# Attention and a mixture of experts: a quarter of GpSimd's descriptor space, and a second result buffer for the large expert blocks

## The chip, the cores and the metric

The kernel runs on one core of a Trainium2 chip, as one program. The metric is the device time of one execution in microseconds, and the median over runs is what is compared. Before the change it is 880.67 us, the median of 3 runs that lie between 877.47 and 881.1 us.

## The reference

Attention over 8 batches, 12 heads, 448 positions and a head dimension of 64, with scores capped by a tanh, and then a mixture of 8 experts in which each of the 3584 tokens goes to one expert alone. All of it is in float32.

```
scores = cap * tanh(q @ k^T / 8 / cap);  attn = softmax(scores);  x = (attn @ v) as [3584, 768]
expert = argmax(x @ w_gate);  g = softmax(x @ w_gate)[expert]
out[token] = g * (relu(x[token] @ w1[expert]) @ w2[expert])     # w1: 768 x 1024, w2: 1024 x 768
```

## The kernel before

The first half of the program is attention, written out by hand step by step: for each of the 48 pairs of heads TensorE makes scores, ScalarE takes tanh and exp, VectorE and GpSimd add up the denominators. A batch's rows of x go to DRAM (`xd`), and GpSimd scatters the token numbers into lists by expert (`place_d`, the tile `ids`).

The second half is the experts. The tokens are processed in blocks, each of one expert: two early blocks (-1 and -2) that begin while attention ends, then five large blocks of 448 slots (0 to 4) and two small ones of 256 slots (10 and 11). For a block GpSimd issues one gather of token numbers (`load_ids`), 14 gathers of 128 rows of x into `xg` (`load_x`; 8 for a small block) and four gathers of weights, 1.5 MB each (`load_w`). ScalarE and VectorE split each chunk of weights into a high and a low part (`high`, `low`), and x as well (`split_xs`), so that three fast products stand for one in float32. TensorE does `up(j, f)`, 18 products into `ph`, and `down(j, f)`, 18 products into the six PSUM tiles `y` for a large block, for f from 0 to 7. They are interleaved, with `up` two steps ahead of `down`. After each `up`, ScalarE writes the high half of the hidden layer, and VectorE the low half (`hb`, L945 and L946).

When the last `down` of a block is done, `evac(j)` moves `y` to SBUF: six transposes on VectorE into the tile `ys` (L1003). They stand in VectorE's order ahead of the two L946 of the next block, whose `up(0)` and `up(1)` TensorE does in the meantime. `put(j)` is 14 scatters from `ys` to the output in DRAM, issued by GpSimd in between the gathers for the block after next, spread over the next block's steps (`moves`, with `PS` and `XS`; `step` is a small GpSimd copy that holds GpSimd back until a given `hb` is there). So the scatters of block j end late in the following block, and `evac` of that block writes `ys` again.

`ys` has one buffer in the pool `wb`. Blocks -1, -2, 0, 1, 2, 3 and 4 and the last small block write it; block 10 puts its result into `xg`. The pool `wb` is opened when attention is over, over the places of attention's tiles, and holds in this order: `w24`, `w25h`, `ys`, `w26l`, `w25l`, `w26h`, `w27`. Pools on the left side begin behind the descriptor space of GpSimd's DMAs, which takes the first 16,384 bytes of each partition; pools on the right side (`xp`, `xq`, `hw`, `hw2`, `rpool`) are counted from the other end. A tile that lies where an older tile of a closed pool lay waits for that tile's last users (`reuse_waits`).

GpSimd's DMAs rotate through eight completion semaphores. In the built program a DMA waits for the one before it on its semaphore, so at most eight are under way, and an instruction that has to wait for all 14 scatters waits for all eight semaphores, two in each of four event-semaphore instructions.

Of the kernel before, what the change touches and what calls it, by code (L numbers as in the profile page):

```python
# [4 lines left out]
F32 = mybir.dt.float32  # L5
# [18 lines left out]
QB = S // 32  # L24

KM = 384
XW = DM // 4
# [99 lines left out]
def attention_moe(tc, qT, kT, vL, capd, wgL, w1a, w1b, w2a, w2b, cst, cmk, out):  # L127
    nc = tc.nc
# [662 lines left out]
    def large(j):  # L791
        return j < NL
# [109 lines left out]
    m = {}  # L902
# [83 lines left out]
    ys = {}  # L986

    def evac(j, cs=range(2)):
        y = m["y"]
        if cs[0] == 0:  # L990

            ys[j] = (
                ys0
                if j == -1
                else xg.rearrange("p q x -> p (q x)")
                if j == ORDER[-2]
                else m["yo"].tile([128, QB * XW], F32, name="ys")
            )
        o = ys[j]
        if large(j):  # L1000
            ov = o.rearrange("p (q k i) -> p q k i", k=KC, i=32)
            for k in range(KC):
                V.transpose(out=ov[:, :, k, :], in_=y[k][:, 0:LARGE].rearrange("p (q j) -> p q j", j=32))  # L1003
        else:
            ov = o[:, 0 : 2 * DM].rearrange("p (c a k i) -> p c k a i", c=2, a=4, i=32)
            for c in cs:
                for half in range(2):
                    src = y[2 * c + half][:, 0:384].rearrange("p (k a i) -> p k a i", a=4, i=32)
                    dst = ov[:, c, 3 * half : 3 * half + 3]
                    if half == 0:  # L1010
                        A.copy(out=dst, in_=src)
                    else:
                        V.tensor_copy(out=dst, in_=src)
# [202 lines left out]
    wb = m["yo"] = pools("wb", **tw)  # L1216
    w2s[4] = chunk(wb, "w24")
    w25h = wb.tile([128, DM], F32R, name="w25h")
    ys0 = wb.tile([128, QB * XW], F32, name="ys")
    w26l = wb.tile([128, DM], F32R, name="w26l")  # L1220
    w2s[5] = [w25h, wb.tile([128, DM], F32R, name="w25l")]
    w2s[6] = [wb.tile([128, DM], F32R, name="w26h"), w26l]
# [25 lines left out]
    split_w1(2)  # L1248
    down(-1, 7)
    evac(-1)  # L1250
    split_w1(3)
    fill(100)
# [54 lines left out]
    for i, j in enumerate(blocks):  # L1307
# [43 lines left out]
        if n1 is not None:  # L1351
            evac(j)
    evac(j, range(1))
    put(j, range(1))
    for f in range(3, FC):
# [90 lines left out]
```

## Time and profile before

| | |
|---|---|
| median of 3 runs | 880.67 us (877.47 to 881.1) |
| the profiled execution's own time | 879.77 us |
| its span, first to last instruction | 877.8 us |
| busy: TensorE (PE) / VectorE (DVE) / ScalarE (ACT) / GpSimd (POOL) | 830.4 / 556.9 / 483.4 / 460.5 us |
| GpSimd's gathers of x, scatters of results, gathers of weights | 114, 98 + 4, 28 |

The page gives each engine's busy time as a share of the span, then the span in slices, the DMA queues, the chain of work that ended last, and groups of instructions with the idle time of the engine ahead of them and what ended that idle time. Times in a timeline are microseconds from the start of the span. Matmuls are pipelined: one is shown as lasting longer than the distance to the next one's start, so that the distance of the starts is what one costs.

### The profile page before, as it was taken

How to read it: one execution, taken by the hardware profiler on the slowest of the kernel's cores; microseconds unless marked ns; L12 is line 12 of the kernel's file. 1: busy time of each engine (PE TensorE's matmuls, PEld its weight loads, DVE VectorE, ACT ScalarE, POOL GpSimd, SP SyncE). 2: the span in 40 equal slices, each digit the busy share in tenths (PEclk: the TensorE clock that was granted, in tenths of full speed). 3: DMA queues.
4: the chain of work that ended last, by engine and by line, in shares of the span. 5: the costliest groups of instructions: out<-in, count | busy, mean ns of one | idle time of the engine just before them, and what ended most of it. 6: DMA issues, size and time to landing. Idle time of an engine off the chain costs nothing.

```text
span 877.8 us, 12128 instructions
## 1 busy us (share of the span) xinstructions
PE 830.4 (95%) x4492; PEld 555.2 (63%) x4492; DVE 556.9 (63%) x912; ACT 483.4 (55%) x573; POOL 460.5 (52%) x380
## 2 busy tenths in 40 slices
PE   8999999999969999689999999999999999999993
PEld 3233332323222322169999989899999999999993
DVE  3559797979966899958682844734635536437620
ACT  7999998989876989413342532423323324233420
POOL 1423353434347654534348767578577675665710
PEclk9999999999999999899999999999999999999997
DMA  6131545555556655336645272454431124544210
GB/s 211 69 127 66 186 80 172 98 154 101 187 100 200 223 162 136 80 93 163 134 167 206 77 300 61 176 193 165 169 100 55 33 63 175 186 180 166 81 43 34
DMA packets 46883, 117.96 MB, mean 134 GB/s; under 512 B 8241, under 2 KB 27091, under 8 KB 43744
## 3 DMA queue, kind: packets, MB, share of 16 engines
q1 hardware_dynamic: 30688, 57.01, 23.5%
q0 software_dynamic: 15840, 59.86, 19.3%
q8 instruction: 37, 0.61, 0.3%
q14 instruction: 30, 0.25, 0.1%
q10 hardware_dynamic: 288, 0.23, 0.1%
HBM read 101.40 MB, written 22.36 MB: 141 GB/s over the span
## 4 chain that ended last, share of the span: by engine, by line
PE 53%; DVE 8%; issue 4%; POOL 2%; DMA 2%; ACT 1%; POOLq 0%; DVEq 0%; ACTq 0%
PE ph L940 23%; PE y L970 17%; PE y L978 4%; DVE p L282 2%; PE po L320 2%; PE sp L253 2%; DVE ys L1003 1%; PE po L970 1%; PE z L970 1%; DMA idt<-ids,ti 1%; POOL out L812 1%; DMA ids<-tok,slots 1%; DVE xl L917 1%; PE ps_l L970 1%; PE ps_s L970 1%
## 5 line engine op out<-in xcount | busy, mean ns | idle before, releaser
L290 POOL TENSOR_TENSOR p<-p,pr 64x896 f32<-64x896 f32 x47 | 107.3, 2282 | 189.8 <-DVE p L282 114.7
L945 ACT ACTIVATE hb<-ph 128x448 fp32r<-128x448 f32 (+1 forms) x69 | 35.1, 508 | 285.9 <-PE ph L940 197.4
L946 DVE SCALAR_TENSOR_TENSOR hb<-ph,hb 128x448 fp32r<-128x448 f32 (+1 forms) x69 | 39.4, 574 | 191.2 <-ACT hb L945 191.2
L264 ACT ACTIVATE pt<-sp,qsc 128x896 f32<-128x896 f32 x144 | 139.2, 1001 | 33.6 <-PE sp L253 33.0
L802 POOL DMA_INDIRECT xg<-xd,xi x114 | 136.5, 1198 | 37.8 <-issue 31.7
L253 PE MATMUL sp<-qr,kr 64*128 64x448 f32 x576 | 134.9, 572 | 3.0 <-ACT pr L264 1.5
L273 ACT ACTIVATE pt<-pt,capt 128x1792 f32<-128x1792 f32 x94 | 132.9, 1413 | 2.3
L320 PE MATMUL po<-pt,vr 128*64 128x448 f32 x576 | 130.9, 562 | 0.0
L812 POOL DMA_INDIRECT out<-ys,xi x98 | 107.7, 1099 | 29.2 <-issue 27.4
L253 PEld LDWEIGHTS sp<-qr,kr 64*128 64x128 f32 x576 | 47.1, 185 | 85.3 <-issue 46.7
L282 DVE TENSOR_TENSOR p<-pt 128x896 f32<-128x896 f32 x48 | 71.3, 1485 | 31.1 <-ACT pt L273 25.5
L320 PEld LDWEIGHTS po<-pt,vr 128*64 128x64 f32 x576 | 33.2, 137 | 79.3 <-issue 78.8
L282 DVE TENSOR_TENSOR p<-p,pt 128x896 f32<-128x896 f32 x48 | 54.5, 1135 | 20.7 <-ACT pt L273 19.8
L544 POOL DMA_INDIRECT ids<-tok,slots x32 | 36.4, 1136 | 12.6 <-issue 5.8
L913 ACT CAST xh<-xt 128x448 fp32r<-128x448 f32 (+1 forms) x54 | 27.0, 531 | 20.8 <-DVE xt L910 20.7
L336 DVE COPY ot<-po 128x448 f32<-128x448 f32 x48 | 29.5, 615 | 10.4 <-PE po L320 10.2
L309 PE MATMUL po<-pr,vr 64*64 64x448 f32 x192 | 27.3, 570 | 7.1 <-DVE ot L336 7.1
L802 POOL DMA_INDIRECT w1r<-in_w1b,widx x7 | 10.0, 1435 | 44.8 <-DVE w17l L848 44.5
L910 DVE STREAM_TRANSPOSE xt<-xg 128x448 f32<-128x448 f32 (+1 forms) x54 | 30.2, 584 | 0.8
L917 DVE TENSOR_TENSOR xl<-xt,xh 128x448 fp32r<-128x448 f32 (+1 forms) x54 | 28.8, 559 | 0.0
L1003 DVE STREAM_TRANSPOSE ys<-y 128x448 f32<-128x448 f32 x36 | 19.8, 613 | 13.2 <-DMA out<-ys,xi 7.7
L952 POOL COPY pace<-hb 128x1 f32<-128x1 f32 x40 | 13.7, 342 | 27.0 <-ACT hb L945 26.9
(420 smaller groups left out, 1946.1 us busy)
## 6 DMA issues: line engine op xcount, KB each, us to landing
vr<-in_vL SPq DMA_DIRECT2D x24, 448.0 KB, 6.1
kr<-in_kT SPq DMA_DIRECT2D x23, 448.0 KB, 3.4
qr<-in_qT SPq DMA_DIRECT2D x23, 448.0 KB, 4.6
xd<-yt SPq DMA_DIRECT2D x20, 336.0 KB, 6.5
xd<-w2r SPq DMA_DIRECT2D x12, 336.0 KB, 6.8
w1r<-in_w1a SPq DMA_DIRECT2D x8, 384.0 KB, 5.3
w1r<-in_w1b SPq DMA_DIRECT2D x8, 384.0 KB, 5.7
w2r<-in_w2a SPq DMA_DIRECT2D x8, 384.0 KB, 5.6
```

The lines of the kernel that those rows point to most:

```text
L253: PE.matmul(sp[:, j, 0:S], kr[r, i, c], qr[r, i, :], start=True, stop=True)
L264: A.activation(out=x, in_=sp[:, 0:2, 0:S], func=AF.Tanh, scale=qsc)
L273: A.activation(out=pt[:, lo:hi, :], in_=pt[:, lo:hi, :], func=AF.Exp, scale=capt)
L282: V.tensor_tensor(out=p4, in0=pt[:, 0:2] if half == 0 else p4, in1=pt[:, 2 * half + 2 : 2 * half + 4], op=ALU.add)
L290: e.tensor_tensor(out=p4[r], in0=p4[r], in1=rests[n // 2][r], op=ALU.add)
L320: PE.matmul(po[64 * j : 64 * j + 64, 0:S], vr[:, n % 2 * 6 + 3 * j + t, :], pt[:, 2 * t + j], start=n == t == 0, stop=t == 2 and n > 0,)
L802: G.indirect_dma_start(out=dst, out_offset=None, in_=src, in_offset=bass.IndirectOffsetOnAxis(ap=idx.bitcast(U32), axis=0), bounds_check=b ...
L812: i = G.indirect_dma_start(out=dst, out_offset=bass.IndirectOffsetOnAxis(ap=idx.bitcast(U32), axis=0), in_=src, in_offset=None, bounds_che ...
L917: e.tensor_tensor(out=m["xl"][:, k, 0:n], in0=xts.pop((j, k)), in1=m["xh"][:, k, 0:n], op=ALU.subtract)
L940: PE.matmul(ph, w[:, c], x[:, k, 0:n], start=i == 0, stop=i == 3 * KC - 1)
L946: V.scalar_tensor_tensor(out=hl, in0=ph, scalar=0.0, in1=hh, op0=ALU.max, op1=ALU.subtract)
L970: PE.matmul(y[k][:, 0:LARGE], w[:, c], h, start=f == 0 and i == 0, stop=f == FC - 1 and i == 2)
```

## The change

The descriptor space is set to 4096 bytes instead of the default 16,384, and `ys` gets two buffers of 10,752 bytes in the pool `wb`. Both lines that allocate `ys` name the same tile, so that they rotate through the same two buffers.

```
@@ evac @@
-                else m["yo"].tile([128, QB * XW], F32, name="ys")
+                else m["yo"].tile([128, QB * XW], F32, name="ys", bufs=2)
@@ attention_moe, the pool wb @@
-    ys0 = wb.tile([128, QB * XW], F32, name="ys")
+    ys0 = wb.tile([128, QB * XW], F32, name="ys", bufs=2)
@@ kernel @@
-    nc = bacc.Bacc("TRN2", target_bir_lowering=False, num_devices=1)
+    nc = bacc.Bacc("TRN2", target_bir_lowering=False, num_devices=1, dynamic_dma_scratch_size=4096)
```

## Rows read from the trace of the kernel before

**Rows 1.** Stretches: length, each engine's busy time, TensorE clock, DMA share, GB/s
```profile
445.00:868.00 423.00, 415.90 (x2182) 386.97 (x2180) 213.97 (x331) 142.98 (x232) 270.12 (x259) 1.00 0.38 136
562.00:620.00 58.00, 56.88 (x281) 52.32 (x280) 29.33 (x43) 18.72 (x30) 41.04 (x39) 1.00 0.43 155
```

**Rows 2.** TensorE's waits from 430 us on: in total, times, longest
```profile
PE y L970 <- DVE hb L946: 1.9, 2, 1.1
PE y L978 <- DVE hb L946: 1.2, 1, 1.2
PE ph L940 <- DVE xl L917: 0.2, 1, 0.2
```

**Rows 3.** Waits of all engines from 440 to 868 us
```profile
POOL w1r L802 <- DVE w17l L848: 44.5, 6, 8.6
...
DVE ys L1003 <- DMA out<-ys,xi: 7.7, 3, 3.7
...
DVE ys L1003 <- PE ph L940: 2.9, 1, 2.9
```

**Rows 4.** Line 1003's event semaphores at three evacuations: durations in ns, first and last start
```profile
L1003 DVEq EVENT_SEMAPHORE  x4: 50/50/3869, 558.2 to 562.5; - x4
...
L1003 DVEq EVENT_SEMAPHORE  x4: 49/50/3152, 617.8 to 621.2; - x4
...
L1003 DVEq EVENT_SEMAPHORE  x4: 50/50/2101, 792.9 to 794.1; - x4
```

**Rows 5.** Timeline of VectorE at three evacuations: start, us, idle time before in brackets
```profile
501.89 0.95 DVE L848 TENSOR_TENSOR w25l<-w2r,w25h 128x768 fp32r<-128x768 f32 x1
502.76 3.29 DVE L1003 STREAM_TRANSPOSE ys<-y 128x448 f32<-128x448 f32 x6
...
562.59 3.31 DVE L1003 STREAM_TRANSPOSE ys<-y 128x448 f32<-128x448 f32 x6 [3.70 <-DMA out<-ys,xi]
565.82 1.12 DVE L946 SCALAR_TENSOR_TENSOR hb<-ph,hb 128x448 fp32r<-128x448 f32 x2
...
796.29 3.30 DVE L1003 STREAM_TRANSPOSE ys<-y 128x448 f32<-128x448 f32 x6 [2.92 <-PE ph L940]
```

**Rows 6.** Timeline of GpSimd: scatters ahead of the evacuations
```profile
552.95 1.62 POOL L812 DMA_INDIRECT out<-ys,xi  x1 [0.30 <-issue]
...
559.51 0.98 POOL L812 DMA_INDIRECT out<-ys,xi  x1 [0.30 <-issue]
...
793.06 1.15 POOL L812 DMA_INDIRECT out<-ys,xi  x1 [0.30 <-issue]
```

**Rows 7.** Timeline of TensorE at the first products of `down` behind three evacuations
```profile
557.49 0.36 PE L970 MATMUL y<-hb,w27l 128*128 128x448 f32 x1
...
564.98 0.36 PE L970 MATMUL y<-hb,w20h 128*128 128x448 f32 x1
566.46 0.47 PE L970 MATMUL y<-hb,w20h 128*128 128x448 f32 x1 [1.12 <-DVE hb L946]
...
566.97 0.57 PE L970 MATMUL y<-hb,w20h 128*128 128x448 f32 x2
...
624.82 0.80 PE L970 MATMUL y<-hb,w20h 128*128 128x448 f32 x2
...
793.75 0.36 PE L970 MATMUL y<-hb,w27l 128*128 128x448 f32 x1
...
798.45 0.33 PE L978 MATMUL y<-w20l,hb 128*128 128x384 f32 x1
799.96 0.62 PE L978 MATMUL y<-w20h,hb 128*128 128x384 f32 x2 [1.18 <-DVE hb L946]
```

**Rows 8.** DMA issues, us to landing; the last line is that of the `w2` gathers
```profile
xg<-xd,xi POOLq DMA_INDIRECT x114, 3.4
out<-ys,xi POOLq DMA_INDIRECT x98, 2.4
...
DMA to landing us min/median/max: 2.1/9.8/10.3
```

## The prediction, made before the result was known

> **What bounds the kernel now.** I read the stretches first. In the expert part, from 445 us to 868 us, TensorE is busy 415.9 of 423 us at a granted clock of 1.00, that is at its upper level of 2.4 GHz, and no other engine comes near: GpSimd 270 us, VectorE 214 us [rows 1]. So only TensorE's own waits can be got back there. The list of them is the second view: three from VectorE's `hb` (1.9 us in two, 1.2 us in one) and one of 0.2 us from `xl`, 3.3 us in all [rows 2]. Everything that a second result buffer could give has to come out of these and of waits too small to be listed. A GpSimd that waits costs nothing by itself.
>
> The third view is who VectorE waits for. Of its time ahead of the transposes of `evac`, 7.7 us are put down to the scatters out of `ys`, 2.9 us to TensorE [rows 3]. The second needs care. Each evacuation is preceded by four event semaphores, two of the scatters' eight completion counts each; a normal one takes 50 ns, and one took 3869 ns at the evacuation from 558 us, 3152 ns from 618 us, and 2101 ns from 794 us [rows 4]. That is the scatters' wait, whatever name is printed. At 559.51 us GpSimd began the last scatter of block -2 and had issued it by 560.49 us; the transposes began at 562.59 us [rows 5, 6]. At 793.06 us it began the last one of block 3, done issuing at 794.21 us, and the transposes began at 796.29 us: the same distance of 2.1 us. I therefore count the wait at 794 us as one for the scatters too.
>
> **The change part by part.**
>
> *The second buffer takes the scatters' wait away.* `evac(j)` then writes the buffer that block j-2's scatters read, and these were issued a whole block (58 us) earlier; they land in 2.4 us [rows 8]. What is late next, at each place:
>
> At 562 us: the last product into `y` starts at 557.49 us [rows 7], and VectorE has nothing left to do from 558.89 us (562.59 - 3.70) [rows 5]. The transposes, 3.31 us, could run from 558.9 to 562.2 us, and the first `hb`, half of 1.12 us, until about 562.8 us [rows 5]. TensorE needs that `hb` for the second product of `down`. Two such products take 0.57 us and one 0.36 us, so their starts are 0.21 us apart, and it would have started at 564.98 + 0.21 = 565.19 us; it started at 566.46 us [rows 7]. Gain 1.27 us, with over 2 us to spare.
>
> At 621 us: two products took 0.80 us instead of 0.57 us [rows 7], a wait too short to be listed. Gain 0.23 us.
>
> At 796 us: block 10 is small, and its two `up` are shorter, so the same delay hits harder. The product due some 0.18 us after 798.45 us (half its printed length, as above) started at 799.96 us [rows 7]: 1.33 us. Without the scatters' wait the transposes start when `y` is done, at 794.11 us (793.75 + 0.36), and with 3.30 us for them and 0.56 us for the first `hb` it is 797.97 us, ahead of 798.63 us. Gain 1.33 us.
>
> At 502 us nothing goes: VectorE was in `w25l` until 502.84 us (501.89 + 0.95), and the transposes followed at once [rows 5]. The smaller of the two waits that make 1.9 us, 0.8 us, is this one and stays [rows 2]. The other two evacuations into `ys` have no wait of TensorE behind them, and nothing is gained there.
>
> The sum is 1.27 + 0.23 + 1.33 = 2.83 us. Bounds: 0, if something else is late at each place; 3.3 us plus 0.5 us (the unlisted 0.23 us, and starts that slip by more than the listed idle time), if every wait of TensorE in the expert part went. It carries to the end, because between the boundaries TensorE's list has no wait [rows 2] that a boundary's delay could hide in.
>
> *Earlier transposes move what follows them.* The splits of `w17`, `w26` and `w27` behind `evac` come up to 3.4 us earlier, and GpSimd's gather of the next weights, which waits 44.5 us in six times for `w17l` [rows 3], goes with them. Nothing on TensorE was waiting for either; I take 0. The other side: VectorE now works beside the last scatters. A scatter beside VectorE's splits took 1.62 us, one without 0.98 us [rows 6], so one or two of them per block may take 0.64 us longer. GpSimd has 58 - 41 = 17 us to spare in a large block [rows 1], and nobody waits for these scatters any more. Cost 0; if it had no slack, 5 x 1.3 = 6.4 us.
>
> The Trainium skill ("SBUF — State Buffer", section "SBUF: two separate sides") says that GpSimd can't write its descriptors while VectorE runs an operation that takes the shared port pair. That would be the reason for the 1.62 us; by that rule alone the change makes GpSimd's issue slower than before, and the sum would still be the same as long as the slack holds.
>
> *The smaller descriptor space.* The trace of before can't show a full one. From below: nothing to gain, since an issue takes 0.98 us with the large space and the engine isn't what bounds. From above: GpSimd waits whenever the space is full. What is under way at once is bounded twice. The program lets eight DMAs be under way, and the slowest gather lands in 10.3 us [rows 8] while issues are 1.3 us apart (0.98 + 0.30) [rows 6], which is eight as well. So the question is whether a quarter holds eight. I take that it does, cost 0; the price if not is the second rival's.
>
> The skill ("DMA: Bandwidth & Descriptors", sections "Terms" and "The descriptor swizzle") gives 16 bytes a descriptor and nine per DMA engine for a transfer over 128 partitions. An estimate from that: 4096 / 16 / 9 = 28 such DMAs, more than three times eight. No run here shows the figure, and the sum doesn't rest on it.
>
> *Tiles move.* All pools on the left begin 12,288 bytes lower, and what stands behind `ys` in `wb` lies 10,752 bytes deeper in attention's old tiles: `w26l`, `w25l`, `w26h` and `w27` leave the places of `yt` (whose last use is the store of x and block -1's first hidden chunks) and go to those of attention's outputs and values, which are dead earlier. The right-hand pools `hw` and `hw2` come to lie over the last pairs' probabilities and sums. Their last readers are TensorE products that stand ahead of block -1's `up(1)`, before any of these tiles is written. Cost 0; from above, a split that waited for one `up` would lose 18 starts of 0.21 us, 3.8 us, once.
>
> **Sum.** The profiled execution's own time is 879.77 us; less 2.83 us that is 876.9 us. The median of the runs is 0.90 us above it, so I forecast 880.67 - 2.83 = 877.8 us.
>
> **Rivals.**
>
> *The gain is smaller, because the name printed at 796 us is right* (2.9 us "PE ph" [rows 3]): then only 1.27 + 0.23 us go, 879.2 us. Against it stands the 2101 ns of the event semaphore. *Or nothing shows*, since VectorE or the next thing is late anyway, as at 502 us: 880.7 us. That the change doesn't do what it says (the four semaphores still wait for the newest scatters, their counts being shared) ends there too. Against it: counts wait for a number, and block j-2's is reached long before.
>
> *The descriptor space is too small for what is under way, and GpSimd waits in the middle of its queue* (the other side). Suppose that a DMA takes so much of it that two fit. Then each small DMA, 2.4 to 3.4 us to landing [rows 8], gives an issue every 1.2 to 1.7 us instead of 1.3, up to 0.4 us more for 28 of them, 11 us; and behind each of the two pairs of weight gathers GpSimd stands about 8 us longer (9.8 us to landing against two issues), 16 us. That is 27 us in a block with 17 us of slack: 10 us late, in five large blocks 50 us, some 928 us. It decides from the point where a block's GpSimd work grows by more than 17 us, that is by 0.5 us for each of its 33 DMAs; below it, nothing. For it: it is the only thing that the change takes away. Against it: it would need a DMA to take an eighth of the quarter or more, and GpSimd's issues in the present kernel show no pause that a space being reused would leave (0.30 us between issues, first and last).
>
> *Faster by more than TensorE's waits allow*: it would have to come from attention, where the change adds no buffer. What speaks for it is only the runs' own spread: the fastest lies 3.2 us below the median. 875 us.
>
> **How the numbers follow.** The forecast 0.62; the half gain 0.14; nothing 0.10; the small space or a moved tile 0.06; faster 0.08. I call it faster or slower beyond 0.5%, 4.4 us, about what a measurement of this kernel can tell from no change: below 876.3 us or above 885.1 us. The forecast lies 1.5 us inside, and runs spread by 3.6 us, so it may fall under the line in about one case in eight: faster 0.62 / 8 + 0.08 = 0.16, slower 0.07, within 0.77. The range goes from the fastest run less the sum, 877.47 - 2.83 = 874.6 us, to the slowest run with no gain and a little lost, 882.0 us.
>
> **What would show it.** The event semaphores ahead of line 1003 at 50 ns each; no wait of VectorE for scatters there; `y L970 <- hb` down to one wait of 0.8 us near 502 us, and `y L978 <- hb` gone; GpSimd's issues at 1.0 us and 0.30 us apart as now. Wrong would be: GpSimd idle in front of gathers with a DMA as releaser, `xg` landing later, or TensorE waiting for `xl` or for a split at a boundary where it didn't.

## The result, and the profile after

The changed kernel takes 871.09 us, median of 7 runs (868.57 to 873.85); the kernel before, run beside it, 877.86 us (7 runs, 875.05 to 881.1). The ratio is 0.9916, with a 95% interval from 0.9889 to 0.9943. The forecast was 877.8 us, and the range ended at 874.6 us: the measured time lies below the whole range. The kernel before also came out 2.81 us lower than the 880.67 us of its first three runs, so the change is worth 6.77 us by the medians, against 2.83 us forecast. The profiled execution took 868.57 us, its span is 866.7 us. Against the profiled execution of before (877.8 us) that is 11.1 us, and they lie in three places.

**At the boundaries of the large blocks, 2.8 us.** The stretches of [rows 1], in the changed kernel (length, busy time of TensorE, of its weight loads, of VectorE, ScalarE and GpSimd with the number of instructions, TensorE's clock, DMA share, GB/s):

```profile
445.00:868.00 423.00, 413.00 (x2171) 385.38 (x2170) 212.34 (x324) 143.18 (x232) 269.25 (x258) 0.99 0.38 136
562.00:620.00 58.00, 58.00 (x287) 53.57 (x286) 29.56 (x43) 19.16 (x30) 40.34 (x39) 1.00 0.44 157
```

In the second line TensorE is now busy for the whole 58 us (56.88 before). The first line now reaches past the end of TensorE's work. What is left of its list of waits in the expert part, [rows 2] before:

```profile
PE y L970 <- DVE hb L946: 1.1, 1, 1.1
PE ph L940 <- DVE xl L917: 0.2, 1, 0.2
```

Line 1003 has two event semaphores left in the whole program, where the kernel before had 24, those of [rows 4] among them, and neither is longer than 50 ns:

```profile
L1003 DVEq EVENT_SEMAPHORE  x2: 50/50/50, 437.1 to 437.2; - x2
```

VectorE's timeline at two of the evacuations of [rows 5], where no idle time in brackets stands ahead of the transposes any more:

```profile
557.05 3.29 DVE L1003 STREAM_TRANSPOSE ys<-y 128x448 f32<-128x448 f32 x6
560.35 0.62 DVE L946 SCALAR_TENSOR_TENSOR hb<-ph,hb 128x448 fp32r<-128x448 f32 x1
...
789.84 3.30 DVE L1003 STREAM_TRANSPOSE ys<-y 128x448 f32<-128x448 f32 x6
793.36 0.42 DVE L946 SCALAR_TENSOR_TENSOR hb<-ph,hb 128x256 fp32r<-128x256 f32 x1 [0.22 <-ACT hb L945]
```

And TensorE's first products of `down` behind the three evacuations of [rows 7]:

```profile
563.16 0.57 PE L970 MATMUL y<-hb,w20h 128*128 128x448 f32 x2
...
621.76 0.57 PE L970 MATMUL y<-hb,w20h 128*128 128x448 f32 x2
...
795.19 0.51 PE L978 MATMUL y<-w20h,hb 128*128 128x384 f32 x2
```

Two products at an undisturbed 0.57 and 0.51 us each time. Putting the same product of both traces side by side, the changed kernel is 1.99 us ahead at 393 us, 3.10 us at 566 us and 4.77 us at 800 us, that is 2.78 us won between the first and the last. Not every microsecond of it falls at a boundary: the lead shrinks to 2.6 us in between and grows again, because TensorE's distance from one product to the next differs by some thousandths of a microsecond between the two traces. At the three places themselves the lead jumps by 1.27, some 0.2 and 1.3 us.

**At the end of the program, 6.1 us.** The last product ends at 863.81 + 0.34 = 864.15 us before, 13.65 us ahead of the end of the span; after the change it ends at 858.96 + 0.34 = 859.30 us, 7.40 us ahead of it. The prediction says nothing of what lies behind the last product. There GpSimd's sequencer (the part that hands an engine its instructions) still has two things to do. The other engines' closing instructions wait for it: in the kernel before, those of TensorE, ScalarE and VectorE start at 877.2 us, just behind the end of the long DRAIN. These rows list the instructions of a line; `x1: a/b/c` are the shortest, the median and the longest in ns, then the first and the last start. In the kernel before:

```profile
L1364 POOLq INC_SWDGE_SEM  x1: 1575/1575/1575, 869.7 to 869.7; - x1
...
L1442 POOLq DRAIN  x3: 40/107/5710, 871.3 to 877.6; - x3
```

In the changed kernel:

```profile
L1364 POOLq INC_SWDGE_SEM  x1: 368/368/368, 864.6 to 864.6; - x1
...
L1442 POOLq DRAIN  x3: 40/107/810, 865.0 to 866.4; - x3
```

1575 + 5710 = 7285 ns have become 368 + 810 = 1178 ns. I call their sum **the end** from here on. It is 6.1 us of the 11.1, and TensorE's last product moves 6.25 us nearer to the end of the span.

**In attention, 2.0 us**, won by 393 us. At 389.5 us the changed kernel is only 0.6 us ahead. The other 1.4 us come from TensorE's clock: from 390 to 393 us it was granted the lower of its two levels (0.50, that is 1.2 GHz) in the kernel before, and the upper one (2.4 GHz) in the changed kernel. The stretch, and the same product of the expert part behind it, before and then after:

```profile
390.00:393.00 3.00, 3.00 (x10) 2.61 (x9) 2.86 (x8) 0.30 (x1) 2.40 (x4) 0.50 0.64 193
...
393.20 0.37 PE L940 MATMUL ph<-xh,w13h 128*128 128x448 f32 x1
```

```profile
390.00:393.00 3.00, 3.00 (x16) 2.63 (x14) 2.81 (x10) 0.30 (x1) 1.96 (x2) 1.00 0.76 207
...
391.21 0.37 PE L940 MATMUL ph<-xh,w13h 128*128 128x448 f32 x1
```

In a later profile of the changed kernel the lower level does fall there (0.68 on average from 390 to 393 us, then 0.50 for a microsecond). So this varies from one execution to the next, and I count nothing of it for the change.

By the mechanisms the change is thus worth 6.1 + 2.8 = 8.9 us. The medians give 6.8 us; 8.9 us is a ratio of 0.9899, inside the interval.

### The profile page after: what moved, and what is told of

Read it like the earlier page. It is cut to its first block, busy times and chain, and to the rows that moved or that the text cites. A ratio compares the mean times of both kernels' runs of the same rounds, so it can differ in the third digit from the quotient of the medians.

```text
span 866.7 us, 12121 instructions
## 1 busy us (share of the span) xinstructions
PE 831.0 (96%) x4492; PEld 555.4 (64%) x4492; DVE 559.2 (65%) x912; ACT 483.6 (56%) x573; POOL 460.4 (53%) x380
## 4 chain that ended last, share of the span: by engine, by line
PE 56%; DVE 8%; DMA 3%; issue 2%; POOL 1%; ACT 1%; POOLq 0%; DVEq 0%; ACTq 0%
PE ph L940 24%; PE y L970 20%; PE y L978 4%; PE po L320 2%; PE sp L253 2%; DVE p L282 2%; DMA idt<-ids,ti 1%; DMA w2r<-in_w2b 1%; DMA ids<-tok,slots 1%; DVE ys L1003 1%; PE po L970 1%; PE z L970 1%; DVE xl L917 1%; PE po L309 1%; DVE yt L505 0%
## 5 line engine op out<-in xcount | busy, mean ns | idle before, releaser
L812 POOL DMA_INDIRECT out<-ys,xi x98 | 107.7, 1099 | 29.2 <-issue 26.4
L282 DVE TENSOR_TENSOR p<-pt 128x896 f32<-128x896 f32 x48 | 76.2, 1587 | 31.9 <-ACT pt L273 25.5
L264 ACT ACTIVATE pr<-sp,qsc 128x896 f32<-128x896 f32 x24 | 23.9, 996 | 5.8 <-PE sp L260 5.2
```

The costliest lines, as they stand in the source:

```text
L264: A.activation(out=x, in_=sp[:, 0:2, 0:S], func=AF.Tanh, scale=qsc)
L282: V.tensor_tensor(out=p4, in0=pt[:, 0:2] if half == 0 else p4, in1=pt[:, 2 * half + 2 : 2 * half + 4], op=ALU.add)
L812: i = G.indirect_dma_start(out=dst, out_offset=bass.IndirectOffsetOnAxis(ap=idx.bitcast(U32), axis=0), in_=src, in_offset=None, bounds_che ...
```

## The experiments

They ran on several chips; each is compared with the kernel before on its own chip. On two of the chips every kernel is slower: the kernel before has medians of 891.42 and 891.02 us there, against 877.86 us beside the result and 877.01 and 879.52 us on the others. Which chip a run met can be told from the median that it is compared with.

### Each half alone, and both again

The smaller space alone:

```diff
-    nc = bacc.Bacc("TRN2", target_bir_lowering=False, num_devices=1)
+    nc = bacc.Bacc("TRN2", target_bir_lowering=False, num_devices=1, dynamic_dma_scratch_size=4096)
```

> The descriptor space of 4096 bytes alone, one result buffer. Theory (the end of the program): with 16,384 bytes GpSimd's last two steps, INC_SWDGE_SEM and DRAIN, took 1.575 + 5.710 = 7.29 us, with 4096 bytes 0.368 + 0.810 = 1.18 us; they depend on the space alone, so 1.18 us here again, the evacuations wait for the scatters as before (event semaphores of 2 to 4 us at three of them), TensorE's waits for hb stay at 3.1 us, and the time is 6.1 us below the kernel before. Rival (the second buffer makes the end short, since nothing is pending on it any more): 7.3 us at the end, and the time of the kernel before within 1 us. Second rival (the smaller space also makes attention 2 us faster): 8 us below.

Measured: 884.2 us (879.22 to 887.62, 7 runs) against 891.42, ratio 0.9915 [0.9876, 0.9954]. Its end, and its waits behind 430 us:

```profile
L1364 POOLq INC_SWDGE_SEM  x1: 368/368/368, 883.1 to 883.1; - x1
...
L1442 POOLq DRAIN  x3: 40/107/810, 883.5 to 884.9; - x3
```

```profile
DVE ys L1003 <- DMA out<-ys,xi: 7.7, 3, 2.6
...
PE y L970 <- DVE hb L946: 1.5, 2, 1.3
PE y L978 <- DVE hb L946: 0.8, 1, 0.8
```

The end is that of the changed kernel, to the nanosecond, and the scatters' waits are those of before. So the gain at the end comes from the smaller space and has nothing to do with the second buffer. The second rival, a faster attention, gets no support: in its profile this kernel is at 400 us 1.4 us behind the kernel before on the same chip. The time, 7.2 us below (4.1 to 11.1 by the interval), can't tell 6.1 us from 8 us by itself. The same kernel once more, later:

> The smaller space alone (4096 B, one result buffer) on another chip than the first time. Theory (two separate gains): the end of the program gives 6.1 us and the waits of the large scatters stay, so 871 to 872 us where the kernel before has 877.5, and INC_SWDGE_SEM plus the last DRAIN take 1.18 us. Rival (the second buffer carries the gain): within 1 us of the kernel before.

Measured: 884.08 us (876.26 to 890.99, 9 runs) against 891.02, ratio 0.991 [0.9875, 0.9945]; the end again 368 + 810 ns. Expected were 6.1 us; measured were 6.9 (medians) or 8.0 (ratio). The interval (0.0055 to 0.0125 of 891: 4.9 to 11.1 us) holds all three, and the rival, under 1 us, falls. The absolute 871 us was wrong, since the run met a slower chip.

Both parts with the largest space that still leaves room for two buffers:

```diff
-    nc = bacc.Bacc("TRN2", target_bir_lowering=False, num_devices=1, dynamic_dma_scratch_size=4096)
+    nc = bacc.Bacc("TRN2", target_bir_lowering=False, num_devices=1, dynamic_dma_scratch_size=7552)
```

> Two result buffers with the largest space that leaves room for them, 7552 bytes. Theory: the end lies on the line between 1.18 us at 4096 and 7.29 us at 16,384 bytes, 1.18 + 3456 x 6.11 / 12288 = 2.9 us, and TensorE's waits are those of the changed kernel; 4.4 + 2.8 = 7.2 us below the kernel before. Rival (the second buffer makes the end short): 1.2 us at the end and 8.9 us below. Rival (the end has a step somewhere, not a slope): 7.3 us or 1.2 us.

Measured: 876.08 us (871.75 to 883.41, 6 runs), ratio 0.983 [0.9787, 0.9873].

```profile
L1364 POOLq INC_SWDGE_SEM  x1: 428/428/428, 873.1 to 873.1; - x1
...
L1442 POOLq DRAIN  x3: 40/107/1055, 873.6 to 875.2; - x3
```

The end takes 1.48 us, not the 2.9 us of my straight line between 4096 and 16,384 bytes. The line was wrong; a law in the size that isn't straight was still open. The whole time was a miss as well, 15.3 us below the kernel before where 7.2 were expected (see "What stays open"). The two kernels unchanged, as a measure of how far executions differ:

> The changed kernel once more, for its profile and on one chip with the others. Theory: end 1.18 us, 6.1 + 2.8 = 8.9 us below the kernel before. If attention too has become faster by the change, up(-1,3) is reached 2 us earlier than in the kernel before again (391.2 against 393.2 us in the first pair), and the time is 11 us below.

> The kernel before once more, for a second profile. Theory: end 7.3 us again; the place where block -1's up(-1,3) starts, 393.2 us in the first profile, lies 1 us or more away from it, because that part of attention varies between executions by itself. Rival (the change made attention faster by 2 us): it lies within 0.5 us of 393.2 us, and the changed kernels' near 391.2 us.

Measured: the changed kernel 876.75 us (876.17 to 879.17, 6 runs), ratio 0.9833 [0.9807, 0.986]; the end 368 + 810 ns. The kernel before 887.38 us, the end 1575 + 5710 ns, as in the first trace. At 400 us its products started within 0.1 us of the first trace's (at 393 us 0.9 us earlier, because the stretch at the lower clock lies a microsecond later), so my expectation that it would lie a microsecond or more away was a miss. The changed kernel did lie apart: at 400 us 1.9 us ahead of before the first time, 0.3 us behind it this time.

On this chip one buffer and two were both run in 4096 bytes, and their profiles give the second buffer's part by itself: two buffers lead one by 1.09 us at 400 us and by 3.49 us at 815 us, which is 2.4 us between, against 2.83 us forecast. No run has one buffer in 4096 bytes on a quieter chip, so the medians don't separate the two parts there.

### Does the end go by the DMAs or by the size?

Without the gathers of x and without the large blocks' scatters (the results of the large blocks are not written, and x is not gathered), 73 DMAs of GpSimd instead of 285, in the space of before:

```diff
-        for g in gs or range(groups(j)):
+        for g in list(gs or range(groups(j)))[:0]:
...
-            for g in gs:
+            for g in list(gs)[:0]:
```

> The kernel before (16,384 bytes, one buffer) without the gathers of x and without the scatters of the large blocks' results, so that GpSimd issues 73 DMAs in place of 285; the experts work on rows that were not loaded. Theory A (the end goes through the DMAs that the space still remembers; at nine descriptors of 16 bytes per DMA engine a space of 16,384 bytes holds 113 of them, 4096 bytes hold 28): only 73 are left to go through, and GpSimd's last INC_SWDGE_SEM and DRAIN take clearly less than 7.29 us, between the 1.48 us of 52 (7552 bytes) and 7.29 us of 113, some 3 to 4 us. Rival (the end clears the space by its size): 7.29 us again. The time itself says nothing here.

```profile
L1364 POOLq INC_SWDGE_SEM  x1: 1654/1654/1654, 865.7 to 865.7; - x1
...
L1442 POOLq DRAIN  x3: 40/107/6037, 867.4 to 874.0; - x3
```

7.69 us, a little more than with 285 DMAs. The theory expected 3 to 4 us. I concluded that the end goes by the size and not by the DMAs. The last group of experiments shows that this conclusion was wrong. Two more sizes, 12,288 bytes with one buffer and 1024 bytes with two:

> The kernel before with 12,288 bytes, one buffer. So far the end took 1.18 us at 4096, 1.48 us at 7552 and 7.29 us at 16,384 bytes, which is no straight line. If it bends gradually: about 4 us here. If there is a step between 7552 and 16,384 bytes: 2 us or 7 us. Theory A has 85 DMAs here and asks for a value above that of the kernel with 73 DMAs; the rival asks for the value by size whatever that one shows.

> Two result buffers and a space of 1024 bytes. At nine descriptors per DMA and engine it holds seven, one less than the eight that the program lets be under way. Theory: the end takes some 0.9 to 1.0 us (1.18 us less 21 DMAs at 0.0125 us, the slope between 4096 and 7552 bytes), GpSimd stands a few us more in a block behind the weight gathers, covered by its 17 us of slack, and the time is that of the changed kernel within 1 us. Rival (a DMA takes more of the space than nine descriptors, so that only two or three fit): GpSimd's issues in a large block come later, xg lands late, TensorE waits for xl, and the time is 20 us or more above the changed kernel.

```profile
L1364 POOLq INC_SWDGE_SEM  x1: 1155/1155/1155, 867.3 to 867.3; - x1
...
L1442 POOLq DRAIN  x3: 40/107/3995, 868.5 to 873.0; - x3
```

```profile
L1364 POOLq INC_SWDGE_SEM  x1: 328/328/328, 865.2 to 865.2; - x1
...
L1442 POOLq DRAIN  x3: 40/107/647, 865.6 to 866.9; - x3
```

Measured: 875.34 us with 12,288 bytes (one run), its end 5.15 us, which is none of the three values expected (4, 2 or 7 us); 870.49 us with 1024 bytes (868.15 to 874.7, 6 runs) against 877.01, ratio 0.9928 [0.9901, 0.9956], its end 0.98 us. The changed kernel beside them:

> The changed kernel beside the one with 1024 bytes, on the same chip. Theory: 8.9 us below the kernel before where TensorE meets no throttle; on the second chip, where TensorE stalled from 823 us on for 3.5 to 13 us in every profile, more than that if two buffers shorten the stall, 8.9 us if the stall's length varied by itself. The profile shows the stall's length once more.

Measured: 871.43 us (867.56 to 872.89, 6 runs), ratio 0.9921 [0.9895, 0.9947]. The 5.6 us below the kernel before are less than the expected 8.9, but the interval (4.6 to 9.2 us) holds both. A sixteenth of the space is no slower than a quarter, and there the time in which GpSimd stands ahead of its gathers of x with nothing named that it waits for is that of before (30.5 us after 31.7).

### Where a small space begins to cost, and two sizes between

512 bytes with two buffers; 8192 and 10,240 bytes with one:

```diff
+    nc = bacc.Bacc("TRN2", target_bir_lowering=False, num_devices=1, dynamic_dma_scratch_size=512)
```

> Two buffers and 512 B of space. If the space still holds what is under way: the end takes 0.95 us and the time is within 2 us of the changed kernel's. The prediction's rival (the space holds too few DMAs, and GpSimd waits in issuing them, from half a microsecond per DMA on): tens of microseconds more, above 890 us, with GpSimd's DMA issues late and SP, VectorE or TensorE waiting for gathered x.

Measured: 924.61 us (918.29 to 927.75, 4 runs) against 891.02, ratio 1.0361 [1.0302, 1.0421], and the shortest end of all. Some of its waits, over the whole program (engine, what waited, for what: us in all, times, longest), then its end:

```profile
POOL xg L802 <- issue: 72.3, 102, 4.2
...
POOL p L290 <- DMA ids<-tok,slots: 27.1, 4, 8.3
...
PE ps_s L358 <- POOL p L290: 19.3, 5, 4.7
```

```profile
L1364 POOLq INC_SWDGE_SEM  x1: 248/248/248, 923.8 to 923.8; - x1
...
L1442 POOLq DRAIN  x3: 40/107/320, 924.1 to 925.3; - x3
```

So the rival of the prediction is real, one halving below 1024 bytes: GpSimd waits in issuing gathers 72.3 us (31.7 before). But it decides in another place than I had it. By 390 us, in attention, the kernel is 36 us behind the first trace of before; the expert part, where I had put all of it, adds some 10 us by 834 us. In attention GpSimd's additions of probabilities stand behind its scatters of `ids` (27.1 us of waiting after 12.7), and TensorE waits 19.3 us for these additions, a wait that isn't in the list of before.

> 8192 B, one buffer. Where the bend in the end's time lies: by the line through 1024, 4096 and 7552 B INC_SWDGE_SEM plus the last DRAIN take 1.5 us, by the line through 12,288 and 16,384 B 3.0 us. Everything ahead of the end as before.

> 10,240 B, one buffer. By the line of the small spaces the end takes 1.7 us, by the line of the large ones 4.1 us; a value between them would be a bend within this stretch. Everything ahead of the end as before.

8192 bytes, then 10,240 bytes:

```profile
L1364 POOLq INC_SWDGE_SEM  x1: 915/915/915, 879.6 to 879.6; - x1
...
L1442 POOLq DRAIN  x3: 40/107/3015, 880.5 to 884.1; - x3
```

```profile
L1364 POOLq INC_SWDGE_SEM  x1: 708/708/708, 884.6 to 884.6; - x1
...
L1442 POOLq DRAIN  x3: 40/107/2198, 885.4 to 888.1; - x3
```

Measured: 886.25 and 890.51 us, one run each. The ends are 3.93 and 2.91 us: the larger space has the shorter end. No law in the size alone gives that, and both of my lines fall.

### What the end counts

The DRAINs differ from one another by whole multiples of 81.7 ns: 647 - 320 = 4 x 81.7, 810 - 647 = 2 x 81.7, 1055 - 810 = 3 x 81.7, and so on up to 6037 - 5710 = 4 x 81.7. INC_SWDGE_SEM moves with them by 20 ns a step. Something is counted. Suppose that the run with few DMAs in 16,384 bytes counts all of its 73; then the end is 0.26 us + 0.102 us x the count, and 512 bytes count 3, 1024 bytes 7. This suggests that a DMA keeps its place in the space after it has landed; only when the space is full are the finished ones freed, and the end goes through those that still have a place. The prediction's estimate from the Trainium skill ("DMA: Bandwidth & Descriptors", sections "Terms" and "The descriptor swizzle") gives what a space holds, 3 DMAs in 512 bytes and 7 in 1024, 28 in 4096, 113 in 16,384; the first two agree with those counts, and no count below is above its space's figure.

The kernel before then fills 113 places twice. If f DMAs are still under way each time it is freed, 285 - 113 - (113 - f) + f = 59 + 2f are left at the end; the end says 69, so f = 5. The same sum gives f = 6 at 12,288 bytes, 6.2 at 8192 and 10,240, 6.5 at 7552, 6.8 at 4096. The number of fillings is taken so that f comes out between 0 and 8, the most that the program lets be under way; at 4096 bytes a smaller number of fillings would do as well, with f = 5. One number is fitted in each, so this needed runs that could contradict it. Four keep the size and change only the number of DMAs. The first two do the scatters of `ids` in attention a second (and a third) time:

```diff
+    idu = dpool.tile([(E + 1) * T, 1], I32, name="idu")
+    idv = dpool.tile([(E + 1) * T, 1], I32, name="idv")
...
+        for grp, dst in (("ids", ids), ("idu", idu), ("idv", idv))[: 2]:
```

The second has `[: 3 if q < 3 else 2]` in place of `[: 2]`, so that 24 of the 32 are done a third time. The third leaves the large blocks' scatters out, the fourth is the run with few DMAs in 4096 bytes.

> The kernel before (16,384 B, one buffer) with each of the 32 scatters of ids in attention done a second time, into a tensor nobody reads: 317 GpSimd DMAs instead of 285. Theory (a DMA stays in the space after it has landed; only when the space is full are the finished ones freed, and the end goes through those still kept, 82 ns in the DRAIN and 20 ns in INC_SWDGE_SEM for each, besides 0.26 us): the kernel before ends with 69 kept, this one with 92 to 101, so 9.6 to 10.6 us. Rival (the end goes by the size of the space): 7.3 us as before.

> As the last, with 24 of them done a third time: 341 GpSimd DMAs, still 16,384 B and one buffer. Theory: the space has been full and freed once more shortly before the end, 6 to 17 are kept, and the end takes 0.9 to 2.0 us, though the space is that of before and the DMAs are more. Rival (by size): 7.3 us.

> The kernel before without the 98 scatters of the large blocks (their part of out is not written): 187 GpSimd DMAs, 16,384 B. Theory: full and freed once, 77 to 80 kept, the end takes 8.1 to 8.4 us, more than before with 98 DMAs fewer. Rival (by size): 7.3 us. TensorE's waits at the boundaries go too, about 2.8 us, which is not the question here.

> 73 GpSimd DMAs as in the run of few DMAs (the gathers of x and the large scatters left out), but in 4096 B. Theory: full and freed two or three times, 17 to 27 kept, the end takes 2.0 to 3.0 us, more than the 1.18 us that 285 DMAs take in the same space. Rival (by size): 1.18 us.

The four ends in this order (in the first two kernels the lines are three lower in the file):

```profile
L1367 POOLq INC_SWDGE_SEM  x1: 2155/2155/2155, 908.3 to 908.3; - x1
...
L1445 POOLq DRAIN  x3: 40/107/8078, 910.5 to 919.5; - x3
```

```profile
L1367 POOLq INC_SWDGE_SEM  x1: 488/488/488, 979.6 to 979.6; - x1
...
L1445 POOLq DRAIN  x3: 40/107/1300, 980.2 to 982.0; - x3
```

```profile
L1364 POOLq INC_SWDGE_SEM  x1: 1735/1735/1735, 865.9 to 865.9; - x1
...
L1442 POOLq DRAIN  x3: 40/107/6363, 867.7 to 874.6; - x3
```

```profile
L1364 POOLq INC_SWDGE_SEM  x1: 734/734/734, 863.0 to 863.0; - x1
...
L1442 POOLq DRAIN  x3: 40/107/2280, 863.7 to 866.6; - x3
```

| run | bytes | GpSimd DMAs | the end, us | kept, by 0.26 + 0.102 x kept | expected to be kept |
|---|---|---|---|---|---|
| 512 bytes | 512 | 285 | 0.57 | 3 | |
| 1024 bytes | 1024 | 285 | 0.98 | 7 | |
| the change | 4096 | 285 | 1.18 | 9 | |
| few DMAs | 4096 | 73 | 3.01 | 27 | 17 to 27 |
| both, 7552 | 7552 | 285 | 1.48 | 12 | |
| 8192 bytes | 8192 | 285 | 3.93 | 36 | |
| 10,240 bytes | 10,240 | 285 | 2.91 | 26 | |
| 12,288 bytes | 12,288 | 285 | 5.15 | 48 | |
| before | 16,384 | 285 | 7.29 | 69 | |
| few DMAs | 16,384 | 73 | 7.69 | 73 (supposed) | |
| no large scatters | 16,384 | 187 | 8.10 | 77 | 77 to 80 |
| 32 more | 16,384 | 317 | 10.23 | 98 | 92 to 101 |
| 56 more | 16,384 | 341 | 1.79 | 15 | 6 to 17 |

All four counts lie in the ranges that the theory gave, two of them at the edge (77 and 27; the 3.01 us are a hair above the 3.0 us that I wrote), and none at what the size alone would give (7.3 us three times, 1.18 us once). With 24 more DMAs the end falls from 10.23 to 1.79 us in the same space, and with 73 DMAs it is longer in 4096 bytes than with 285. It also explains the earlier run that misled me: 16,384 bytes keep all 73. The freeing itself isn't seen as a row; it is inferred from these counts. In the kernel before, the 114th DMA, the first that would find 113 places taken, is issued in 1.00 us and 0.30 us behind the one before it, like its neighbours. The whole times of these four (921.86, 984.34, 877.02 and 868.63 us, one run each, against 879.52 before) say nothing on it: the added scatters hold GpSimd up in attention, and leaving work out moves other things.

## Why the prediction was wrong

**The step that failed** is the one on the smaller descriptor space: "From below: nothing to gain, since an issue takes 0.98 us with the large space and the engine isn't what bounds." It was priced at 0, and it measured 6.1 us, more than twice the whole forecast gain. I looked for the space's price only where DMAs are issued. The price lies where the program ends, and it stood in the trace of before, 7.3 us long, on GpSimd's sequencer behind the last work. The views that the prediction rests on end at 868 us. Others that I had asked for reach to 880 us, but none has a row behind GpSimd's last scatter, done at 866.5 us, since what a sequencer does by itself isn't counted as work there. I didn't ask what filled the 11 us of span behind that row.

With this term the sum would be 2.83 + 6.1 = 8.9 us. From the 880.67 us that the prediction started from, this gives 871.7 us, close to the median of 871.09; but that is luck in part, since the kernel before measured 877.86 us beside the changed one, and from there it gives 868.9 us.

**The boundaries** were right: 2.83 us forecast, 2.78 us found, the event semaphores at 50 ns, the 1.1 us near 502 us the only wait for `hb` left (forecast 0.8). The name TensorE at 796 us was indeed wrong and the scatters' semaphore right. With one buffer in 4096 bytes, these waits stay. Place by place the gains came out as forecast, too (1.27, 0.23 and 1.33 us forecast; 1.27, some 0.2 and 1.3 found).

**Earlier transposes and moved tiles** cost nothing, as forecast: GpSimd's busy time is 460.4 us after 460.5, and VectorE's splits wait no longer than before (0.3 us each). The prediction's other side didn't come either: the 98 scatters took 107.7 us in both traces. Its reading that a scatter beside VectorE's splits takes 1.62 us was too general, for the scatter just before that one, at 551.67 us, ran beside the split of `w16` and took 0.97 us. So the scatters' times neither bear out nor refute the rule that the prediction cites for them: no run shows which of VectorE's operations would shut them out.

**The rival of the small space** had a real mechanism. Its 928 us, for room for two DMAs, look close to the 924.61 us measured with room for three, but that is luck: it had 47 us lost, and 33.6 us were lost on a chip where before takes 891.02. It was also wrong in where it bites, mostly attention instead of the expert part. That a quarter has room enough was right; a sixteenth still has.

**The rival of more than TensorE's waits allow** pointed the right way, since 875 us was nearest. But it looked for the source in attention and in the spread of the runs, and gave it 0.08.

**What stays open.** Measured gains on the two quieter comparisons are 6.8 and 5.6 us, below the 8.9 of the mechanisms, though 8.9 lies in both intervals. On the first of the slower chips it was 14.7 us, more than the mechanisms give. There the engines are held up near 830 us, which isn't seen on the quieter chips. Set beside the first trace of before, the two kernels with two buffers and at least 4096 bytes lost 5.4 and 7.1 us from 815 us to the end, the six others on the slower chips 8.6 to 13.8 us. Two kernels are too few to say that the change does this.

## What to carry to other kernels

Read the span to its last instruction: the time behind the last work belongs to some engine's sequencer, and a change to a resource that it cleans up can be worth more there than in the loop. An end that counts leftovers goes up and down with the number of DMAs as well as with the space, so a step that adds or removes DMAs can move the time by microseconds at a place where it changed nothing. And an experiment that varies one quantity at one level can hide a law that saturates there, as 73 DMAs did in a space that holds 113.

## What the runs showed that I had not expected

**Two executions of attention.** Near 344 us GpSimd's addition of probabilities starts either a moment ahead of two products of VectorE, which then take 2.91 us instead of 1.02, or 1.5 us behind their start. GpSimd's row and VectorE's, in the first trace of before, then in the third series of the changed kernel:

```profile
345.14 2.08 POOL L290 TENSOR_TENSOR p<-p,pr 64x896 f32<-64x896 f32 x1
...
343.67 1.02 DVE L436 TENSOR_TENSOR lt<-lt,rr 64x448 f32<-64x448 f32 x2
```

```profile
343.81 2.07 POOL L290 TENSOR_TENSOR p<-p,pr 64x896 f32<-64x896 f32 x1
...
343.85 2.91 DVE L436 TENSOR_TENSOR lt<-lt,rr 64x448 f32<-64x448 f32 x2
```

TensorE behind it waits 1.37 us for VectorE in the one and 3.42 us in the other. The changed kernel showed both cases in its three profiles, so this is no fixed effect of the change. The two profiles of the kernel before have the later case only; too few to say whether a smaller space makes the earlier one more frequent. It isn't the source of the 2.0 us of attention in the first pair: both traces of that pair have the 1.02 us. The Trainium skill ("SBUF — State Buffer", section "SBUF: two separate sides") describes a pair of ports that GpSimd and VectorE share and that one of them holds for a whole instruction; the 2.91 us agree with one waiting for the other, though no run here takes GpSimd's addition away.

**A pause on two chips.** On the slower chips TensorE, ScalarE and VectorE lose 5 to 14 us in one stretch, in most of the runs between 825 and 840 us, while GpSimd goes on issuing. In the smaller space alone, run again, TensorE starts its products 0.7 us apart from 827 us on, with no wait that the profile names. Then it waits 5.62 us for ScalarE's `hb`, which ScalarE begins after 9.67 us of idle time although the products that it reads were done by 825 us (the profile names "remote" as the releaser, and no instruction). From 830.5 us on, after five microseconds with few products, TensorE was granted the lower of its two clock levels, until 841 us. The stretch (columns as in [rows 1]) and the two rows:

```profile
830.00:835.00 5.00, 0.64 (x2) 0.30 (x2) 0.00 (x0) 0.00 (x0) 2.93 (x3) 0.55 0.23 79
...
835.86 0.38 ACT L945 ACTIVATE hb<-ph 128x256 fp32r<-128x256 f32 x1 [9.67 <-remote]
...
836.29 0.69 PE L978 MATMUL y<-w27h,hb 128*128 128x384 f32 x1 [5.62 <-ACT hb L945]
```

The same stretch in the first trace of before, on a quieter chip:

```profile
830.00:835.00 5.00, 4.84 (x38) 4.51 (x37) 3.06 (x9) 2.38 (x7) 4.08 (x4) 1.00 0.25 82
```

Every profile from the two slower chips has such a pause and none from the others does, the kernel before among both. So it goes with the chip as far as these runs reach; its cause was not found.
